# First loads of x in another order, and all five engine orders searched anew: a four-layer attention and MLP kernel on one core

## Chip, core, metric

The kernel runs on one core of a Trainium2 chip (trn2). The metric is the device time of one execution in microseconds (us). The program is one launch; nothing else runs on the core.

## What is computed

x has 2048 tokens of 448 numbers in bfloat16. Four layers follow one another, and each adds its result to x: attention, MLP, attention, MLP, with the same weights both times.

```python
def _A_ref(x, wqkv, wo):          # H = 16 heads of 28, window W = 8, dilation 2
    qkv = (x @ wqkv) -> q, k, v   # per head
    idx = pos[:, None] - arange(W)[None, :] * 2
    logits = einsum("bhsd,bhswd->bhsw", q, k[idx]) * Dh ** -0.5   # -1e9 where idx < 0
    return (softmax(logits) @ v[idx]) @ wo
def _B_ref(x, w_gate, w_up, w_down):                              # F = 1792
    return ((x @ w_gate) * (x @ w_up)) @ w_down
x = x + _A_ref(_layernorm(x), A_wqkv, A_wo)
x = x + _B_ref(_layernorm(x), B_w_gate, B_w_up, B_w_down)
x = x + _A_ref(_layernorm(x), A_wqkv, A_wo)
x = x + _B_ref(_layernorm(x), B_w_gate, B_w_up, B_w_down)
```

## The kernel before

Tokens are taken apart by parity, so that the dilation disappears: 16 blocks of 128 tokens, blocks 0 to 7 the even ones. Each layer is cut into chunks of 256 or 512 tokens, and the chunks of neighbouring layers are interleaved (`SEQ`: A00 A01 B10 A02 B11 and so on, layer and chunk).

Steps are named here by kind, layer and number. LayerNorm of a block is bn, mv (statistics, VectorE), lnv, rstd (ScalarE) and xn (normalized x, VectorE); T is its transposed form, made in layer 0's opening by a TensorE transpose (L602, L606) and a copy from PSUM on ScalarE or VectorE (L613, L616), later by a DMA. QK is the copy of a K and Q product from PSUM (L701), V and VT that of a V product. S is a group's attention scores (L826), on which an exponential (L835, ScalarE) and a minimum with a mask (L842, VectorE) follow, AV the product with V (L860), Oc and Oa its copies, Rs, Rl, R and N the division by the sum, Y the product with wo. G and H are the MLP's copy and product (L951, L954), Dd its down projection. S-2-14 is the scores of layer 2 for the group of query blocks that ends with block 14, QK-0-3-2 the copy for layer 0, chunk 3, head quarter 2.

All long matrix products go through one helper, so all have line L351. They use TensorE's array as two halves of 64 rows: two matmuls run side by side and make one pass. S and AV are bursts of 16 to 64 small matmuls; from S-0-12 on, S works on the array in columns of 32 like AV. A burst can be cut: `549*1.2.4.5/438` says that burst 549 (64 small matmuls) is cut after 8, 16, 32 and 40 of them, and that after each cut stands one step of long product 438, done as 8 strips of 32 columns (L354) in place of two matmuls, so that the array's division is the same. A number without a star is a step that runs whole. `a+b` is two bursts taken together.

Nothing chooses an order at run time. `ORDER` lists the steps of each engine by number; `BANKS` says which PSUM banks each product takes, and a product waits until the step that empties a bank has run. Waits on semaphores follow from the steps' dependences alone. The numbers are those in which `build` adds the steps, so a step added earlier or left out shifts all later numbers: after the change the numbers from 56 on are lower by 3.

At the start SyncE issues the loads of x (16 blocks; `load_x`), WV (`wv`), wqkv in four pieces (`stg`), then the MLP's weights. TensorE meanwhile runs `WARM + FILL` = 18 matmuls on zeros (L502), 13 of them ahead of the first transpose. VectorE and ScalarE copy wqkv into a padded form (L510, wqk), and a first QK product needs all eight such copies. The down-projection weights (WD) are loaded around 50 us.

Of the kernel before, what the change touches and what calls it, by code (L numbers as in the profile page):

```python
# [58 lines left out]
FILL = 9  # L59
# [36 lines left out]
def grp_nc(g):  # L96
# [21 lines left out]
    ),  # L118
    "act": (
# [12 lines left out]
    ),  # L132
    "dve": (
# [18 lines left out]
    ),  # L152
    "pool": (
        "18 19 38 20 21 22 23 24 25 26 27 28 29 30 31 32 33 34 35 36 37"
    ),
# [224 lines left out]
def build(nc, A_x, A_wqkv, A_wo, B_w_gate, B_w_up, B_w_down, out):  # L380
# [54 lines left out]
    def one(fn, key=None):  # L435
        return [(fn, key)]
# [14 lines left out]

    load_x(0, 0, 1, prio=-51.0)
    load_x(0, 1, 2, "g", -49.6)
    load_x(0, 2, 4, "h", -49.5)
    def wv_rows(a, lo, hi):
        v = A_wqkv[192 * a:192 * a + 128, lo:hi]
        r = v.ap[0][0]
# [639 lines left out]
```

## Time and profile before

| what | before |
|---|---|
| median of 3 runs, us | 384.83 (384.31 to 384.89) |
| the profiled execution, us | 383.93 |
| its span from first to last instruction, us | 382.2 |
| TensorE busy, us | 376.7 |
| VectorE busy, us | 288.2 |
| ScalarE busy, us | 203.8 |
| granted TensorE clock, mean | 1.000 |

The span is the profiled execution without the launch around it. Busy time of TensorE is modelled to the end of each matmul and these overlap, so starts are the better measure of its pace. In the chain of waits each piece is the time from its start to the start of the next piece of the chain.

### The profile page before, as it was taken

What the parts mean: (1) busy time and instruction counts of PE and PEld (TensorE: products, weight loads), DVE (VectorE), ACT (ScalarE), POOL (GpSimd) and SP (SyncE); (2) the same over time, 40 slices, a digit from 0 to 9 for tenths busy, and PEclk for the clock granted to TensorE, in tenths of its full rate; (3) what the DMA queues carried; (4) which work ended last, traced back from release to release, by engine and by line L of the source; (5) the groups of instructions that cost most, each with busy time, mean ns of one, the idle gap of its engine ahead of it and who ended that gap; (6) DMA issues with size and microseconds to landing.
All of it is one profiled execution on the core that took longest, in us unless ns stands there. A gap on an engine that the chain in (4) does not pass through costs nothing.

```text
span 382.2 us, 14253 instructions
## 1 busy us (share of the span) xinstructions
PE 376.7 (99%) x6322; PEld 211.2 (55%) x6322; DVE 288.2 (75%) x649; ACT 203.8 (53%) x388; POOL 5.2 (1%) x25
## 2 busy tenths in 40 slices
PE   8999999999999999999999999999999999999997
PEld 3545587544445445444756765545555444446664
DVE  7989999998976786787677985637998698455323
ACT  5997896756426552564465525547744635133320
POOL 5000000000000000000000000000000000000000
PEclk9999999999999999999999999999999999999999
DMA  7756454700611033031101035330125004140002
GB/s 248 196 142 160 53 121 116 84 20 2 94 32 36 2 60 62 15 67 26 32 14 34 19 44 101 36 47 4 27 34 74 3 2 66 35 116 30 3 2 98
DMA packets 54881, 22.50 MB, mean 59 GB/s; under 512 B 45012, under 2 KB 54820, under 8 KB 54820
## 3 DMA queue, kind: packets, MB, share of 16 engines
q1 hardware_dynamic: 54676, 21.53, 28.0%
q8 instruction: 50, 0.82, 0.9%
q14 instruction: 11, 0.09, 0.1%
q10 hardware_dynamic: 144, 0.06, 0.1%
HBM read 8.54 MB, written 2.71 MB: 29 GB/s over the span
## 4 chain that ended last, share of the span: by engine, by line
PE 93%; DVE 3%; ACT 1%; DMA 1%; issue 1%; SPq 0%; DVEq 0%
PE ps L351 85%; PE ps L354 3%; PE ps L860 2%; PE ps L826 2%; PE ps L966 1%; DMA x_sb<-in_A_x_dram 1%; DVE xn_sb L592 1%; ACT E_sb L835 1%; DVE Qz L812 0%; DVE R_sb L885 0%; SPq L443 0%; DVE st L571 0%; ACT xnTa L616 0%; PE ps L606 0%; ACT qk L701 0%
## 5 line engine op out<-in xcount | busy, mean ns | idle before, releaser
L351 PE MATMUL ps<-xnTb,WGU 64*128 64x512 bf16 (+1 forms) x1894 | 172.4, 332 | 0.0
L351 PEld LDWEIGHTS ps<-xnTb,WGU 64*128 64x128 bf16 x1894 | 92.3, 94 | 69.2 <-issue 1.0
L951 ACT ACTIVATE g_sb<-ps 128x512 bf16<-128x512 f32 (+1 forms) x140 | 70.2, 509 | 84.4 <-PE ps L351 64.6
L954 DVE TENSOR_TENSOR hT<-g_sb,ps 128x512 bf16<-128x512 bf16 (+1 forms) x140 | 78.2, 574 | 47.1 <-ACT g_sb L951 44.5
L351 PE MATMUL ps<-WD,hT 64*128 64x448 bf16 x812 | 82.9, 349 | 0.0
L351 PEld LDWEIGHTS ps<-WD,hT 64*128 64x128 bf16 x812 | 38.9, 94 | 34.9 <-DVE hT L954 0.4
L351 PE MATMUL ps<-xnTa,WQK 64*128 64x512 bf16 (+1 forms) x494 | 53.1, 352 | 0.4 <-ACT qk L701 0.2
L915 DVE TENSOR_TENSOR x_sb<-x_sb,ps 128x448 bf16<-128x448 bf16 x62 | 37.1, 612 | 13.6 <-PE ps L351 13.4
L835 ACT ACTIVATE E_sb<-ps,shift_sb 128x1024 bf16<-128x1024 f32 (+1 forms) x36 | 37.1, 1067 | 12.6 <-PE ps L826 12.4
L592 DVE TENSOR_SCALAR xn_sb<-x_sb,mv,rstd 128x512 bf16<-128x512 bf16 (+1 forms) x64 | 35.4, 567 | 6.4 <-ACT rstd L576 6.2
L571 DVE BATCH_NORM_STATS2 st<-x_sb 128x6 f32<-128x448 bf16 x64 | 38.5, 615 | 1.1 <-DMA x_sb<-in_A_x_dram 0.7
L351 PEld LDWEIGHTS ps<-xnTa,WQK 64*128 64x128 bf16 x494 | 23.0, 94 | 22.0 <-ACT xnTa L616 0.5
L701 ACT ACTIVATE qk<-ps 128x1024 bf16<-128x1024 f32 (+1 forms) x27 | 25.4, 958 | 16.1 <-PE ps L351 16.0
L351 PE MATMUL ps<-wo_g,oT 64*128 64x448 bf16 x250 | 28.6, 349 | 0.0
L842 DVE TENSOR_TENSOR E_sb<-E_sb,MK 128x1024 bf16<-128x1024 bf16 (+1 forms) x36 | 23.3, 658 | 5.3 <-ACT E_sb L835 5.2
L886 ACT ACTIVATE R_sb<-R_sb 128x480 f32<-128x480 f32 (+1 forms) x34 | 20.2, 600 | 11.1 <-DVE R_sb L885 10.9
L898 DVE TENSOR_TENSOR oT<-O_sb,R_sb 128x480 bf16<-128x480 f32 (+3 forms) x36 | 22.1, 624 | 4.3 <-ACT R_sb L887 4.2
L351 PE MATMUL ps<-WV,xnTa 64*128 64x336 bf16 (+3 forms) x252 | 24.0, 304 | 0.3
L885 DVE STREAM_SHUFFLE R_sb<-O_sb 128x480 f32<-128x480 f32 (+1 forms) x34 | 22.9, 693 | 0.0
L574 ACT ACTIVATE lnv<-mv,eps_sb 128x2 f32<-128x2 f32 (+1 forms) x33 | 9.3, 291 | 22.3 <-DVE mv L573 22.3
L887 ACT ACTIVATE R_sb<-R_sb 128x480 f32<-128x480 f32 (+1 forms) x34 | 20.0, 600 | 0.6
L871 ACT ACTIVATE O_sb<-ps 128x512 f32<-128x512 f32 (+3 forms) x19 | 10.4, 559 | 14.2 <-PE ps L860 14.2
(60 smaller groups left out, 217.8 us busy)
## 6 DMA issues: line engine op xcount, KB each, us to landing
out_dram<-x_sb SPq DMA_DIRECT2D x15, 112.0 KB, 1.8
x_sb<-in_A_x_dram SPq DMA_DIRECT2D x3, 448.0 KB, 6.3
hT<-in_A_wqkv_dram SPq DMA_DIRECT2D x4, 224.0 KB, 4.9
WGU<-in_B_w_gate_dram SPq DMA_DIRECT2D x4, 224.0 KB, 3.5
WGU<-in_B_w_up_dram SPq DMA_DIRECT2D x4, 224.0 KB, 4.1
WD<-in_B_w_down_dram SPq DMA_DIRECT2D x2, 448.0 KB, 4.1
WGU<-in_B_w_gate_dram SPq DMA_DIRECT2D x2, 336.0 KB, 4.5
WGU<-in_B_w_up_dram SPq DMA_DIRECT2D x2, 336.0 KB, 4.4
```

The lines of the kernel that those rows point to most:

```text
L351: return lambda E: E.matmul(out(), lhs(), rhs(), start=start, stop=stop)
L571: sc.add("dve", one(lambda E, B=B: E.bn_stats(st6[:, B, :], x_sb[:, B, :]), ("bn", li, B)), 525.0, deps=[("x", li - 1, B)] + ([("xn", li - ...
L592: sc.add("dve", one(lambda E, B=B, dst=dst, src=src: E.tensor_scalar(dst, src, mv[:, B, 0:1], rstd[:, B:B + 1], ALU.subtract, ALU.mult), ( ...
L701: return E.activation(dst, src, ACT.Copy) if hasattr(E, "activation") else E.tensor_copy(dst, src)
L835: return E.activation(E_sb[:, slot, 2 * hp:2 * hp + 2, 0:w], ps[:, b0:b0 + 2, 0:w], ACT.Exp, bias=shift_sb[:, 0:1], scale=SCALE)
L842: return E.tensor_tensor(e, e, MK[:, kind, 0:nc].unsqueeze(1).unsqueeze(1).to_broadcast([128, 2, w // nc, nc]), ALU.min)
L885: sc.add("dve", one(lambda E: E.stream_shuffle(R_sb[:, rs, 0:w], O_sb[:, os_, 0:w], [DH] * 32), ("Rs", li, qb)), dve_est(w) + 20.0, deps=[ ...
L886: sc.add("act", one(lambda E: E.activation(R_sb[:, rs, 0:w], R_sb[:, rs, 0:w], ACT.Ln), ("Rl", li, qb)), act_est(w, False), deps=[("Rs", l ...
L898: return E.tensor_tensor(oT[:, :, a % HALF:a % HALF + z - a], O[:, :, a - tok:z - tok], R_sb[:, rs, 0:w].rearrange("p (h n) -> p h n", h=4 ...
L915: sc.add("dve", one(lambda E: E.tensor_tensor(x_sb[:, B, :], x_sb[:, B, :], ps[:, bk[w], 0:D], ALU.add), ("x", li, B)), dve_est(D), deps=[ ...
L951: sc.add("act", one(lambda E, gs=gs, bk=bk: E.activation(g_sb[:, gs, 0:nt], ps[:, bk[0], 0:nt], ACT.Copy), ("G", li, j, fc)), act_est(nt), ...
L954: sc.add("dve", one(lambda E, gs=gs, bk=bk, fc=fc: E.tensor_tensor(hT[:, fc, hs, 0:nt], g_sb[:, gs, 0:nt], ps[:, bk[1], 0:nt], ALU.mult), ...
```

## The change

The first loads of x go in the order block 1, block 0, blocks 2 and 3, blocks 4 to 7 (before: 1, 2 and 3, 0, 4 to 7). Six of the filler matmuls of `FILL` remain of nine, 15 in all, 12 of them ahead of the first two transposes. The small constants' memsets are added in a fixed order, the copies `wqp` are VectorE's by declaration (they ran there before too), and `ORDER` and `BANKS` are replaced throughout by lists from a new search, which by the change's own words counted down-projection loads as delaying instruction fetches. The steps themselves are the same but for the three fillers; 19 copies move from ScalarE to VectorE and 22 the other way.

```diff
-FILL = 9
+FILL = 6
...
     "pe": (
-        "41 42 43 44 45 46 47 48 49 50 51 52 53 108 54 55 56 105 57 58 123 206 126 207 236 129 132 237 200 224 201 225 196 230 197 150 231 226 194 227 198 195 "
...
-        "352 365 353 366 498 272 499 375 369 565 370 566 569 570 397 380 304 298 301 310 284 307 285 316 322 334 313 319 392 522 331 393 402 516 325 517 328 "
-        "511 337 512 340 341 544*3.5/342 343 527 584 414 585 415 444 441 453 447 459 539 456 540 549*1.2.4.5/438 468 465 471 450 595*1.3.5/462 477 589 561 474 "
...
-        "1237 1244 1312 1334 1245 1301 1246 1238 1302 1247 1239 1401 1398 1392 1404 1351*1.3.5/1416 1324 1346 1395 1325 1347 1428 1413 1410 1422 "
...
+        "41 42 43 44 45 46 47 48 49 50 51 52 105 102 53 54 55 120 203 123 204 233 129 126 234 197 193 198 221 194 222 195 191 196 227 192 228 225 223 153 144 "
...
+        "399 541*2.4.5/339 513 340 524 581 514 582 411 438 412 444 456 536 450 537 468 462 546*1.2.4.5/441 453 435 465 447 592*1.3.5/474 459 471 477 586 478 "
...
+        "1309+1326*3.5.7.9.11.13/1235 1236 1241 1242 1331*3.5/1298 1243 1244 1299 1395 1398 1410 1348*1.3.5/1389 1321 1401 1392 1404 1322 1422 "
...
-    load_x(0, 0, 1, prio=-51.0)
-    load_x(0, 1, 2, "g", -49.6)
-    load_x(0, 2, 4, "h", -49.5)
+    load_x(0, 1, 2, "g", -51.0)
+    load_x(0, 0, 1, prio=-50.9)
+    load_x(0, 2, 4, "h", -50.8)
+    load_x(1, prio=-50.7)
...
-    memset("dve", eps_sb[:], EPS, "c_eps", 70)
-    memset("dve", wo_g[:], 0.0, "c_wo", 760)
+    first = sc.ops[-1]
+    memset("dve", eps_sb[:], EPS, "c_eps", 70, after=first)
+    memset("dve", wo_g[:], 0.0, "c_wo", 760, after=first)
...
-            sc.add(("pool", "dve"), one(fn, ("wqp", c, w)), {"pool": 240.0, "dve": 115.0}, ...
+            sc.add("dve", one(fn, ("wqp", c, w)), {"dve": 115.0}, ...
```

In the old list 1312 is AV-2-12, 1334 AV-2-14, 1329 (cut three times, in the line ahead of the one shown) S-2-14, 402 AV-0-8 and 544 S-0-12; in the new one 1309 is AV-2-12, 1326 S-2-14, 1331 AV-2-14 and 541 S-0-12, with AV-0-8 (399) right ahead of it.

The bursts whose cuts or neighbours differ, by number of cuts:

| burst | before | after |
|---|---|---|
| AV-0-8, S-0-12 | none; 2, apart | none; 3, neighbours |
| S-0-16, AV-0-16 | 3; 2 | 2; 3 |
| S-2-4 | 1 | 3 |
| AV-2-6 | 3 | 2 |
| AV-2-8 | 3 | 2 |
| S-2-14 | 3, alone | together with AV-2-12, 6 in all |
| AV-2-12, AV-2-14 | none, neighbours | see S-2-14; 2, alone |

Copies that change engines in the opening: T-0-2, T-0-7, T-0-8, T-0-10, QK-0-2-0 and VT-0-0 from ScalarE to VectorE; T-0-4, T-0-12, T-0-13, T-0-15, QK-0-0-2, QK-0-3-2 and QK-0-4-3 from VectorE to ScalarE; two weight copies and two Oc copies change places with two others of their kind. ScalarE's order after rstd of block 5 is T-0-3, two weight copies, V-0-0, T-0-5, T-0-4 (before: T-0-3, two weight copies, T-0-5, and V-0-0 five steps after that). On SyncE the four wqkv pieces go 0, 1, 2, 3 (before 0, 2, 1, 3), x 8 to 11 goes ahead of one further weight load, the ones for vt go ahead of nine weight loads, and the four WD loads go behind a few more stores to vt. GpSimd's order differs in one memset.

More of the change, by code (lines that the diff above doesn't have):

```diff
@@ L104 @@
     "pe": (
[13 rows of a table removed]
[13 rows of a table added]
     ),
     "act": (
[12 rows of a table removed]
[12 rows of a table added]
     ),
     "dve": (
[18 rows of a table removed]
[18 rows of a table added]
     ),
     "pool": (
-        "18 19 38 20 21 22 23 24 25 26 27 28 29 30 31 32 33 34 35 36 37"
+        "18 19 20 21 22 23 24 25 26 27 28 29 30 31 32 33 34 35 36 37 38"
     ),
     "sp": (
[5 rows of a table removed]
[5 rows of a table added]
     ),
@@ L446, in build, with load_x @@
     stage = hT[:].rearrange("p f s n -> p (f s n)")
-    def load_x(q, lo=0, hi=4, tag="", prio=0.0):
+    def load_x(q, lo=0, hi=4, tag="", prio=0.0, after=None):
         two, b0 = q // 2, 4 * (q % 2)
-        plain_dma("sp", x_sb[:, 4 * q + lo:4 * q + hi, :], x_par[two][:, b0 + lo:b0 + hi, :], [("x", -1, B) for B in range(4 * q + lo, 4 * q + hi)], f"d_x{q}" + tag, prio=prio)
-    load_x(0, 0, 1, prio=-51.0)
-    load_x(0, 1, 2, "g", -49.6)
-    load_x(0, 2, 4, "h", -49.5)
+        plain_dma("sp", x_sb[:, 4 * q + lo:4 * q + hi, :], x_par[two][:, b0 + lo:b0 + hi, :], [("x", -1, B) for B in range(4 * q + lo, 4 * q + hi)], f"d_x{q}" + tag, prio=prio, after=after)
+    load_x(0, 1, 2, "g", -51.0)
+    load_x(0, 0, 1, prio=-50.9)
+    load_x(0, 2, 4, "h", -50.8)
+    load_x(1, prio=-50.7)
     def wv_rows(a, lo, hi):
@@ L461, in build @@
         plain_dma("sp", stage[:, 2 * D * c:2 * D * (c + 1)], A_wqkv[CH_ROWS[c]:CH_ROWS[c] + 128, 0:2 * D], ("stg", c), f"d_stg{c}", prio=-49.9)
-    load_x(1, prio=-49.3)
     for a in range(2):
@@ L470, in build, with memset @@
     sc.add("act", one(act_table_load), 1300.0, prio=-61)
-    def memset(eng, ap, val, key, est):
-        sc.add(eng, one(lambda E: E.memset(ap, val), key), est, prio=-40)
+    def memset(eng, ap, val, key, est, after=None):
+        sc.add(eng, one(lambda E: E.memset(ap, val), key), est, prio=-40, after=after)
     memset("dve", warm, 0.0, "c_warm", 100)
-    memset("dve", eps_sb[:], EPS, "c_eps", 70)
-    memset("dve", wo_g[:], 0.0, "c_wo", 760)
+    first = sc.ops[-1]
+    memset("dve", eps_sb[:], EPS, "c_eps", 70, after=first)
+    memset("dve", wo_g[:], 0.0, "c_wo", 760, after=first)
     sc.add("pool", one(lambda E: E.memset(ident[:], 1.0), "i_id"), 150, prio=-46)
@@ L483, in build @@
     memset("pool", shift_sb[:], -SHIFT, "c_shift", 100)
-    memset("pool", MK[:], BIG, "i_mk", 300)
+    memset("pool", ones32[:], 1.0, "c_ones", 100)
+    masks_after = [o for o in sc.ops if o.engs == ("pool",)]
+    for o, prev in zip(masks_after[1:], masks_after):
+        o.after = prev
+    memset("pool", MK[:], BIG, "i_mk", 300, after=masks_after[-1])
     later = [(W - 1 - 64, 1, -1), (64, -1, 1)]
@@ L495, in build @@
     assert HALF - qb_info(STRADDLE)[0] == 64 and STRADDLE % 2 == 0
-    memset("pool", ones32[:], 1.0, "c_ones", 100)
-    sc.add("dve", one(lambda E: E.memset(qmask[:], 0.0), "i_qm"), 60, prio=-39.5)
+    sc.add("dve", one(lambda E: E.memset(qmask[:], 0.0), "i_qm"), 60, prio=-39.5, after=first)
     sc.add("dve", [((lambda E, r=r: E.memset(qmask[32 * r:32 * r + DH, r % 2:r % 2 + 1], 1.0)), "c_qm" if r == 3 else None) for r in range(4)], 240, deps=["i_qm"], prio=-39.5)
@@ L518, in fn @@
                 return E.tensor_copy(dst, src)
-            sc.add(("pool", "dve"), one(fn, ("wqp", c, w)), {"pool": 240.0, "dve": 115.0}, deps=[("stv", c // 2), "c_wqk0"] + [(k, 0, 0, cc) for k in ("Kps", "Qps") for cc in range(4)] + [(k, *NOPW[-1], cc) for k in ("Kps", "Qps") for cc in range(4)], prio=-27.5)
+            sc.add("dve", one(fn, ("wqp", c, w)), {"dve": 115.0}, deps=[("stv", c // 2), "c_wqk0"] + [(k, 0, 0, cc) for k in ("Kps", "Qps") for cc in range(4)] + [(k, *NOPW[-1], cc) for k in ("Kps", "Qps") for cc in range(4)], prio=-27.5)
     WQKR = [(k, c, w) for c in range(4) for w in range(2) for k in ("wqk", "wqp")]
```

119 rows, old and new, of tables (BANKS, ORDER) are left out of this document.

## The prediction

> **What bounds the kernel now.** I read the page first, then the busy time by stretches, then the chain of waits in order of time, and last the timeline of the first 22 us.
>
> ```profile
> span 382.2 us, 14253 instructions
> PE 376.7 (99%) x6322; PEld 211.2 (55%) x6322; DVE 288.2 (75%) x649; ACT 203.8 (53%) x388; POOL 5.2 (1%) x25
> q8 instruction: 50, 0.82, 0.9%
> PE 93%; DVE 3%; ACT 1%; DMA 1%; issue 1%; SPq 0%; DVEq 0%
> ```
>
> TensorE is busy for 376.7 of 382.2 us and holds 93% of the chain. So nearly everything that TensorE no longer does, or no longer waits for, is taken off the end, and a saving elsewhere counts only where TensorE waited for it. Line q8 matters later: 50 fetches of instructions, against 6322 matmuls and 6322 weight loads on TensorE, is one fetch for about 253 instructions of that engine.
>
> ```profile
> core 0: us, PE busy (x) PEld busy (x) DVE busy (x) ACT busy (x) POOL busy (x), PEclk, DMA share, GB/s
> 8.30:11.40 3.10, 2.90 (x61) 1.84 (x60) 3.10 (x13) 3.08 (x9) 0.00 (x0) 1.00 1.08 352
> 20.80:48.40 27.60, 26.51 (x554) 14.32 (x554) 25.95 (x67) 24.22 (x39) 0.00 (x0) 1.00 0.52 111
> 48.40:100.00 51.60, 51.60 (x1060) 32.20 (x1062) 49.25 (x114) 36.79 (x73) 0.00 (x0) 1.00 0.35 69
> 284.00:287.00 3.00, 2.46 (x140) 1.62 (x138) 2.96 (x6) 0.13 (x2) 0.00 (x0) 1.00 0.77 77
> 287.00:380.00 93.00, 92.82 (x1156) 50.56 (x1152) 54.24 (x109) 33.02 (x65) 0.00 (x0) 1.00 0.21 43
> ```
>
> The first two numbers of a row are its length and TensorE's busy time. TensorE idles in three places: a few tenths near the first QK product, 1.09 us between 20.8 and 48.4 (VectorE is busy for 25.95 of those 27.60 us and ScalarE for 24.22, so both are close to full), and 0.54 us at 284 to 287. After 287 it idles for 0.18 us in 93, with ScalarE and VectorE at a third and a little over half: what is won at 285 us reaches the end undiminished. Busy TensorE can still be slow TensorE, and that shows in the chain.
>
> **The bursts and their prices.** Attention's small matmuls (L826 scores, L860 attention times V) come in bursts of 64 and use the array in 32 columns; the long products (L351) use 128. A burst can stand alone, or be cut, with 8 strips of a long product (L354) between its pieces.
>
> ```profile
> 61.90 0.61 PE ps L860 x64
> ...
> 69.87 0.22 PE ps L826 x18
> ...
> 70.71 2.38 PE ps L351 x24
> ...
> 126.94 0.21 PE ps L860 x24
> ...
> 127.76 21.37 PE ps L351 x218
> ...
> 194.06 0.41 PE ps L826 x30
> ...
> 194.81 5.76 PE ps L351 x68
> ...
> 257.95 0.18 PE ps L860 x16
> ...
> 258.95 6.39 PE ps L351 x58
> 265.35 0.15 PE ps L860 x8
> 265.50 0.22 PE ps L354 x8
> ...
> 280.43 0.18 PE ps L826 x10
> ...
> 281.40 3.51 PE ps L351 x36
> 284.91 0.61 PE ps L860 x64
> ...
> 286.23 0.50 issue
> ...
> 286.93 13.77 PE ps L351 x140
> ```
>
> The columns are start, length, what. From a burst's first row to the next L351 row is its whole time; the strips in it are useful work, 0.22 us a step at 512 columns (row 265.50), so 0.19 at 448. What is left is the burst's price. AV alone: 0.61. AV with 3 steps: 1.00 - 0.66 = 0.34 (257.95). AV with 2: 0.82 - 0.44 = 0.38 (126.94). S with 3: 0.97 - 0.57 = 0.40 (280.43). S with 2: 0.84 - 0.38 = 0.46 (69.87). S with 1: 0.75 - 0.22 = 0.53 (194.06). Going into a burst costs again about 0.1, in the piece before it: 36 matmuls of 448 columns are 18 passes, 3.42 us at 0.19, and row 281.40 has 3.51. AV-2-12 and AV-2-14, uncut and back to back, take 284.91 to 286.93 = 2.02 us, 0.50 of which is "issue": TensorE waits in the middle of the second burst for nothing that a semaphore shows. These are 128 matmuls and 128 loads, one whole fetch of the q8 line, run in about 1.5 us; I read it as instructions that had not arrived.
>
> **The change part by part.** The new order lists hold the same long passes; I compared the bursts one by one.
>
> (a) At 280 to 287 us: before, S-2-14 cut by 3 steps, then the uncut pair: 0.40 + 2.02 + two entries of 0.10 = 2.62. After, AV-2-12 and S-2-14 are one burst cut by 6 steps, and AV-2-14 is cut by 2. No row shows AV and S in one cut burst. From above it is two bursts, 0.34 + 0.40 + 0.20 = 0.94; with one way out and one entry fewer it is 0.74, and I go 0.08 lower for the bottom (the pieces may hide more loads). I take 0.74, the sum of its two halves less one switch each way. AV-2-14: 0.38 + 0.10. After: 1.22, gain 1.40 (1.20 to 1.48).
> (b) AV-0-8 alone and S-0-12 with 2 steps, 0.61 + 0.46 + 0.20 = 1.27, become neighbours, S with 3 steps: 0.61 + 0.40 + 0.10, less the way back of 0.10, is 1.01. Gain 0.26 (0.16 to 0.36, one switch more or less).
> (c) S-2-4 goes from 1 step to 3: 0.53 to 0.40, gain 0.13.
> (d) S-0-16 goes from 3 steps to 2 (loss 0.06), AV-0-16 from 2 to 3 (gain 0.04), AV-2-6 and AV-2-8 from 3 to 2 (loss 0.08): loss 0.10.
>
> All others keep their number of cuts. Sum of the bursts: a gain of 1.69 us (1.4 to 1.9).
>
> [...]
>
> **The opening.** These rows are of the timeline and the groups by shape.
>
> ```profile
> 1.25 5.55 PE L502 MATMUL ps<-hT 128*128 128x512 bf16 x13 [1.25 <-DVE eps_sb L473]
> ...
> 4.11 1.68 DVE L571 BATCH_NORM_STATS2 st<-x_sb 128x6 f32<-128x448 bf16 x3 [0.30 <-DMA x_sb<-in_A_x_dram]
> ...
> 8.26 0.29 PE L606 MATMUL ps<-ident,xn_sb 64*128 64x64 bf16 x8
> ...
> 9.79 1.09 ACT L510 ACTIVATE WQK<-hT 128x448 bf16<-128x448 bf16 x2
> ...
> 11.42 3.58 PEld L351 LDWEIGHTS ps<-xnTa,WQK 64*128 64x128 bf16 x48 [0.54 <-ACT xnTa L616]
> ...
> 12.99 0.34 ACT L775 ACTIVATE v_sb<-ps 128x224 bf16<-128x224 f32 x1
> ...
> 13.22 0.26 ACT L780 ACTIVATE v_sb<-ps 128x112 bf16<-128x112 f32 x1
> ...
> 21.40 0.29 PEld L826 LDWEIGHTS ps<-Qz,qk 64*64 64x64 bf16 x16 [0.73 <-ACT xnTa L616]
> ```
> ```profile
> L701 ACT ACTIVATE qk<-ps 128x1024 bf16<-128x1024 f32 x23 | 23.3, 1022 | 14.1 <-PE ps L351 14.0
> ...
> L701 DVE CAST qk<-ps 128x1024 bf16<-128x1024 f32 x5 | 6.1, 1223 | 1.7 <-PE ps L351 1.5
> ...
> L616 ACT ACTIVATE xnTa<-ps 128x512 bf16<-128x512 bf16 x8 | 4.7, 596 | 0.3 <-PE ps L606 0.3
> ...
> L701 DVE CAST qk<-ps 128x512 bf16<-128x512 f32 x4 | 2.7, 682 | 0.0
> ...
> L616 DVE COPY xnTa<-ps 128x512 bf16<-128x512 bf16 x6 | 2.5, 417 | 0.0
> ```
>
> Fillers: 13 run before the first transpose, 0.43 us each; three fewer free TensorE for 0.3 us at most where it waits for normalized x anyway. I count nothing.
>
> Loads of x: with block 0 second, VectorE no longer waits 0.30 us at 4.11 before its statistics; the eps and qmask memsets move behind and fill part of that. The weights that QK needs come after the same bytes as before (x 0 to 7, then WV, then the four pieces), so the first QK product cannot come earlier. On SyncE, pieces 1 and 2 change places, x 8 to 11 passes one weight load, the ones for vt move ahead of nine loads, and the down-projection loads move behind more vt stores: all are needed tens of us later, and the cover is that distance. GpSimd's ones memset moves behind four others, in 5.2 us of work that ends by 7.
>
> First QK: ScalarE's order is now two weight copies, V of block 0, then the transposes T-0-5 and T-0-4. In times of before: 10.88 after the weight copies (9.79 + 1.09), 11.48 after V (0.34 + 0.26), 12.08 after T-0-5. QK's first piece takes V's bank at 11.5, three passes of 256 columns (0.33) later the next piece needs T-0-5's bank and waits from 11.8 to 12.1. Against 11.42 and no such wait before, this loses 0.3.
>
> S-0-0, the wait at 21.40: there ScalarE is late with a transpose's copy. It loses T-0-2, T-0-7, T-0-8 and a 0.26 us V copy and takes T-0-4 and a 512-column QK copy (0.68 on VectorE, no more here): about 0.8 us less before that point, enough to make up the 0.3. I put both at 0 together; the bounds are a gain of 0.4 and a loss of 0.3.
>
> 21 to 48 us: over the opening VectorE gives away T-0-4, T-0-12, T-0-13, T-0-15, QK-0-0-2, QK-0-3-2 and QK-0-4-3 (4 x 0.417 + 2 x 0.682 + 1.223 = 4.26) and takes T-0-2, T-0-7, T-0-8, T-0-10, QK-0-2-0 and a V copy (4 x 0.417 + 1.223 + about 0.3 = 3.19). So 1.07 us leave VectorE, and 0.9 comes to ScalarE (QK-0-0-2 and QK-0-4-3 at 0.6 each as for 512 columns in row 596, QK-0-3-2 against QK-0-2-0 at 1.022 each, less 0.26), which had 3.38 us free in 20.8 to 48.4 against VectorE's 1.65. TensorE idles 1.09 there; I take 0.3 of it as won. Bounds: a gain of 1.1 (all the idle goes), a loss of 0.9 (ScalarE becomes the late one).
>
> **Sum.** -1.69 + 0 - 0.3 = -2.0 us on the profiled execution: span 382.2 to 380.2. That execution took 383.93, and the median of the three runs is 384.83, 0.9 above; I take 2.0 off the median: **382.8**.
>
> **Rivals.** (B) The bursts gain, and the opening gives it back: ScalarE takes VectorE's place as the late engine, +0.9 and +0.3, which leaves -0.5: 384.3. For it: both engines are over 87% busy in 20.8 to 48.4. Against: the wait at 21.40 is on ScalarE, and there it gets less work.
>
> (C) Slower, at 6 to 12 us: with three fillers fewer TensorE stands idle for some 0.7 us around 7.6 (12 fillers from 1.25 end at 6.4, two transposes and three fillers make 7.6, and block 2's transpose did not start before 8.26), and its clock, which rises only during the fillers (13 took 0.43 us each, twice a 512-column step's 0.22), does not rise or falls back. The work at 8.3 to 11.4, 2.90 us, then takes up to 2.9 more. With -2.0 that is +0.9: 385.7. It decides from 2.8 us of lost time on. Against: the waits between fillers and transposes were there before too. [...]
>
> (D) Slower, in 48 to 284 us: the old order leaves TensorE no idle time there at all (51.60 of 51.60 us in the row above), so a new order can only add waits. Eight to ten new ones of 0.3 us, the size of the waits quoted, are 2.8 us: +0.8, 385.6. For it: every list changes. Against: VectorE and ScalarE have slack there after 100 us, and the order of stages is the same.
>
> (E) The fetch comes back: the merged burst is 128 small matmuls and 48 strips with as many loads, 352 instructions in 0.74 + 6 x 0.19 = 1.9 us, denser than one fetch allows if a block's edge falls badly. Price 0.5 to 0.9: 383.3 to 383.7, still faster; it belongs to the forecast's own range, 381.6 to 384.0.
>
> **Chances.** Forecast with E 0.60, B 0.22, C 0.08, D 0.10. A measurement of this kernel can tell 0.2%, 0.77 us, from no change. So faster by more than that 0.60, within it 0.22 (B), slower 0.18 (C and D). The range goes from the forecast's lower end, 381.6, over B to the edge of D, 385.5.
>
> **What would show it.** Right: no "issue" of 0.5 us in the chain near 285, a single stretch of L860, L826 and L354 for AV-2-12 and S-2-14 of about 1.9 us, and 1.3 us or more won between the row of 280 us and the end; TensorE idle in 20.8 to 48.4 under 1.09 us. Wrong: fillers or the first V passes at 0.43 us after 7 us (C); idle TensorE between 48 and 284 (D); S-0-0 or S-0-8 later than 21.4 and 48.4 (B); an "issue" row inside the merged burst (E).

## The result and the profile after

The changed kernel takes 385.85 us (median of 18 runs, 385.29 to 388.42) where the kernel before takes 384.76 (18 runs on the same chip, 384.0 to 386.16): ratio 1.0037, 95% interval 1.0026 to 1.0049. It is slower by 1 to 1.9 us; 2.0 faster was forecast. Its profiled run is the longest of the 18, so a second trace of the same kernel (run *again* below, 385.14 us) is read beside it.

The page of the profiled run, its busy lines and the chain's shares:

```profile
span 386.7 us, 14316 instructions
PE 378.0 (98%) x6355; PEld 209.5 (54%) x6355; DVE 286.5 (74%) x646; ACT 204.7 (53%) x391; POOL 5.2 (1%) x25
PE 92%; DVE 3%; DMA 2%; ACT 2%; SPq 1%; issue 1%; DVEq 0%
```

DMA and SyncE's queue now hold a part of the chain, and TensorE idles more. Where, by the busy time by stretches, first of the profiled run, then of *again* (length, TensorE busy):

```profile
20.80:48.40 27.60, 24.77 (x520) 12.86 (x520) 22.55 (x59) 22.75 (x36) 0.00 (x0) 1.00 0.49 115
48.40:100.00 51.60, 50.79 (x1068) 31.78 (x1066) 48.53 (x112) 35.12 (x70) 0.00 (x0) 1.00 0.35 72
100.00:284.00 184.00, 183.11 (x3096) 99.77 (x3094) 135.01 (x290) 95.01 (x179) 0.00 (x0) 1.00 0.22 37
```
```profile
20.80:48.40 27.60, 26.66 (x551) 14.14 (x554) 24.43 (x63) 24.62 (x38) 0.00 (x0) 1.00 0.48 115
48.40:100.00 51.60, 50.83 (x1058) 31.58 (x1058) 48.66 (x112) 35.22 (x71) 0.00 (x0) 1.00 0.36 74
100.00:284.00 184.00, 183.86 (x3110) 100.12 (x3108) 135.22 (x291) 93.96 (x177) 0.00 (x0) 1.00 0.22 37
```

Between 48 and 100 us, where the kernel before had no idle time, TensorE idles 0.8 us in both. In 20.8 to 48.4 the two traces of one kernel differ by 1.9.

Idle time misses short losses inside "busy" stretches, and orders that differ can't be set side by side step by step. But at many points both orders have run exactly the same set of TensorE steps. The start of the next product there, changed minus before, gives the loss of each stretch, and the rows add up to the end:

| stretch, us of before | forecast | profiled run | *again* |
|---|---|---|---|
| to 26.6 | 0 | -0.17 | -0.28 |
| 26.6 to 41.1 | -0.3 | +2.68 | +0.79 |
| 41.1 to 74.1, with (b) | -0.26 | -0.35 | -0.37 |
| 74.1 to 93.2 | 0 | +0.83 | +0.71 |
| 93.2 to 203, with (c) | -0.11 | +1.88 | +0.74 |
| 203 to 276 | +0.08 | +0.37 | +0.38 |
| 276 to 294.5, with (a) | -1.40 | -1.09 | -1.10 |
| 294.5 to the end | 0 | +0.32 | +0.32 |
| sum | -2.0 | +4.47 | +1.19 |

Most of the gain forecast for the bursts came, 1.1 us of 1.40 for (a) alone; the 0.3 us forecast for 21 to 48 us did not. The losses were not forecast. Three of them can be read in chains. First the profiled run before Y-0-0, then SyncE's DMA issues in it and in *again* (start, length):

```profile
34.45 3.42 DMA wo_g<-in_A_wo_dram
37.87 0.09 issue
37.96 2.13 PE ps L351 x24
```
```profile
28.39 0.60 SPq L443 DMA_DIRECT2D WGU<-in_B_w_up_dram  x1
31.50 2.25 SPq L443 DMA_DIRECT2D wo_g<-in_A_wo_dram  x3
33.79 0.61 SPq L443 DMA_DIRECT2D WGU<-in_B_w_up_dram  x1
34.45 0.58 SPq L443 DMA_DIRECT2D wo_g<-in_A_wo_dram  x1
```
```profile
28.30 1.23 SPq L443 DMA_DIRECT2D wo_g<-in_A_wo_dram  x3
30.21 0.60 SPq L443 DMA_DIRECT2D WGU<-in_B_w_up_dram  x1
30.86 0.58 SPq L443 DMA_DIRECT2D wo_g<-in_A_wo_dram  x1
```

The last quarter of wo stands behind a weight load that waits for an earlier load to land. In *again* it is issued at 30.86 and is there in time; in the profiled run at 34.45, it lands 3.42 us later, and TensorE stands still for over 2 us. Same order, 3.6 us apart. In *again* the chain before Y-0-0 is on ScalarE:

```profile
32.80 0.49 ACT R_sb L891
33.30 0.49 ACT R_sb L890
33.79 0.62 ACT v_sb L797
34.41 0.49 ACT R_sb L891
34.90 0.92 ACT qk L705
...
35.96 2.13 PE ps L351 x24
```

Third, *again* from AV-0-8 to the product for Y-0-6:

```profile
68.38 0.75 PE ps L864 x64
...
69.15 1.03 ACT O_sb L875 x2
...
70.19 2.12 ACT E_sb L839 x2
72.31 0.99 ACT R_sb L890 x2
...
73.32 1.10 ACT R_sb L891 x2
74.42 0.93 ACT O_sb L875 x2
...
75.48 2.61 PE ps L351 x23
```

AV-0-8 now stands right ahead of S-0-12, so its copies and divisions and S-0-12's exponential follow one another on ScalarE: 1.03 + 2.12 + 0.99 + 1.10 + 0.93 = 6.17 us, and 6.3 us with the short pieces between them (69.15 to 75.48). TensorE's own steps behind AV-0-8 are done at 74.96, after 5.8 us, so it waits 0.5 us. The last term copies AV-0-10 out of the bank that the product needs.

The merged burst came as one stretch, as forecast (chain of the profiled run):

```profile
288.32 0.21 PE ps L864 x24
...
290.08 0.14 PE ps L830 x18
290.22 4.27 PE ps L351 x44
294.48 0.21 PE ps L864 x24
...
295.33 1.76 PE ps L351 x17
```

AV-2-12 and S-2-14 are one stretch of 1.90 us with six strip steps of 0.19 and no "issue" in it: a price of 0.76 without the entry, where 0.64 was forecast. AV-2-14 takes 0.85; its two strip steps are of a product of 336 columns, 0.14 each by their columns, which leaves 0.57 where 0.38 was forecast.

### The profile page after: what moved, and what is told of

The parts are those of the page before. It is cut to its first block, busy times and chain, and to the rows that moved or that the text cites. A ratio compares the mean times of both kernels' runs of the same rounds, so it can differ in the third digit from the quotient of the medians.

```text
span 386.7 us, 14316 instructions
## 1 busy us (share of the span) xinstructions
PE 378.0 (98%) x6355; PEld 209.5 (54%) x6355; DVE 286.5 (74%) x646; ACT 204.7 (53%) x391; POOL 5.2 (1%) x25
## 4 chain that ended last, share of the span: by engine, by line
PE 92%; DVE 3%; DMA 2%; ACT 2%; SPq 1%; issue 1%; DVEq 0%
PE ps L351 83%; PE ps L354 3%; PE ps L830 2%; PE ps L864 2%; PE ps L970 1%; DMA wo_g<-in_A_wo_dram 1%; SPq L443 1%; DMA x_sb<-in_A_x_dram 1%; DVE st L575 1%; ACT E_sb L839 1%; DVE R_sb L889 0%; PE ps L610 0%; DVE E_sb L846 0%; DVE xn_sb L596 0%; DVE qk L705 0%
## 5 line engine op out<-in xcount | busy, mean ns | idle before, releaser
L575 DVE BATCH_NORM_STATS2 st<-x_sb 128x6 f32<-128x448 bf16 x64 | 37.5, 614 | 1.6 <-DMA x_sb<-in_A_x_dram 1.2
L596 DVE TENSOR_SCALAR xn_sb<-x_sb,mv,rstd 128x896 bf16<-128x896 bf16 (+1 forms) x64 | 34.9, 567 | 3.0 <-ACT rstd L580 2.0
L705 ACT ACTIVATE qk<-ps 128x1024 bf16<-128x1024 f32 (+1 forms) x29 | 26.8, 936 | 13.6 <-PE ps L351 13.4
L351 PE MATMUL ps<-WV,xnTa 64*128 64x336 bf16 (+3 forms) x248 | 23.2, 304 | 0.1
L351 PEld LDWEIGHTS ps<-wo_g,oT 64*128 64x128 bf16 x252 | 12.1, 94 | 13.1 <-issue 2.4
```

What stands on the lines that cost most here:

```text
L351: return lambda E: E.matmul(out(), lhs(), rhs(), start=start, stop=stop)
L575: sc.add("dve", one(lambda E, B=B: E.bn_stats(st6[:, B, :], x_sb[:, B, :]), ("bn", li, B)), 525.0, deps=[("x", li - 1, B)] + ([("xn", li - ...
L596: sc.add("dve", one(lambda E, B=B, dst=dst, src=src: E.tensor_scalar(dst, src, mv[:, B, 0:1], rstd[:, B:B + 1], ALU.subtract, ALU.mult), ( ...
L705: return E.activation(dst, src, ACT.Copy) if hasattr(E, "activation") else E.tensor_copy(dst, src)
```

## The experiments

For kernels made of parts, `X|t|Y` says that all engines keep X's order up to the TensorE step at time t and Y's from there; the joints were put where both have run the same set of steps, and banks were renamed to fit. b is before, a the changed kernel. Ratios are to before, run alternately on the same chip.

**again**: the changed kernel unaltered.

> The changed kernel once more, unaltered, for a second trace of it. Its 18 runs spread from 385.3 to 388.4 us, and its profiled run was the longest of them. Queue theory (the load of wo's last quarter waits on SyncE behind a gated load of the MLP's weights, and TensorE waits 2.3 us for it before Y-0-0): the wait is there again, 1 to 2.5 us long, and what differs between runs of 385.3 and 388.4 is mostly its length. Fetch theory (the order is denser, so blocks of 256 instructions come late near 200 us): the issue rows of 0.7 and 0.3 us come and go instead, and the wait before Y-0-0 stays at 2.3. Median 385.9 by both.

385.14 to 387.27, median 386.55, ratio 1.0055 (1.0039 to 1.0070). Counted from start to start, 0.39 us are lost right before Y-0-0 against 2.27 in the profiled run (the view of waits has 0.22 and 2.11), and the "issue" near 200 us is 0.10 against 0.72 and 0.12: both vary from run to run, so neither theory holds alone. The profiled run's two rows of "issue" there stand 256 TensorE instructions apart (counted under fillers, below). The profiled 388.42 is the kernel with both.

**a_wo**: wo's last quarter ahead of the gated load, ones for vt last.

```diff
-"sp": "... 79 78 72 81 80 87 85 86 82 88 84 83 294 ..."
+"sp": "... 79 78 81 80 87 85 86 88 82 84 83 72 294 ..."
```

> The changed kernel with two moves on SyncE alone: the fourth wo load ahead of the gated weight load instead of behind it, and the ones for vt behind the last weight load, as before. Queue theory: the wait of 2.3 us before Y-0-0 goes, to 0.3 or less, and of that 1.5 to 2.3 us reach the end: 383.6 to 384.4. Rival, new waits spread over 48 to 284 us are what costs: the time won at 36 us is waited for again at the next tight places (AV-0-4, S-0-8), at most 0.5 us reaches the end: 385.4 or more.

385.43 (385.08 to 386.13), ratio 1.0036 (1.0023 to 1.0049), 1.1 us under *again* at overlapping intervals. All four wo loads go at 29.64 and nothing is left of the DMA wait; Y-0-0 still comes 0.39 us late, behind ScalarE. Without the DMA wait the slow end of the spread is gone: the eleven runs of a_wo and a_wo18 (below) lie in 385.08 to 386.13, where *again* reaches 387.27. Most of the loss is elsewhere, as the rival had it.

**b_wo**: the same in reverse, in the kernel before.

```diff
-"sp": "... 79 82 81 84 83 90 91 89 88 85 86 87 75 297 ..."
+"sp": "... 79 82 81 75 84 83 90 88 89 85 91 87 86 297 ..."
```

> The kernel before with the same part of the change alone: on SyncE the ones for vt ahead of nine loads, and the wo loads in the changed order, the fourth behind the gated weight load. Queue theory: TensorE waits 1.5 to 2.5 us before Y-0-0, and the median goes from 384.8 to 386.3 to 387.2. Rival (the wait came from the other engines' orders): under 385.2.

384.41, ratio 1.0001 (0.9992 to 1.0011): nothing. The last wo load went at 33.2 and Y-0-0 began at 36.7 without a wait. In the old order two more halves of products stand ahead of Y-0-0, and the changed order comes to it at 35.6: it brings Y-0-0 forward *and* its load back. My theory of SyncE alone fell.

**Which stretch?** Four kernels of parts: `b|243|a`, `b|48|a|243|b`, `a|48|b`, `a|28|b`.

```diff
-every list = changed
+b243_a:      before up to 1074, changed from 1125   (243 us)
+b48_a243_b:  changed only from 397 (S-0-8, 48 us) to 1125
+a48_b:       changed up to 397
+a28_b:       changed up to 250 (AV-0-2, 28.6 us)
```

> The kernel before up to the product that follows S-2-8 (243 us), the changed order from there on, on all engines; banks of the second part renamed so that each product finds the bank it expects. It holds the merged burst of AV-2-12 and S-2-14, the cut AV-2-14, the cuts of AV-2-8 and the changed order of the last 140 us. Theory that each stretch's waits are its own: set step by step against before, the second trace of the changed kernel loses 0.3 us from 243 to 277, wins 1.1 from 276 to 295 and loses 0.3 after it, so 0.5 us faster than before. Rival, what is won at 285 us is there only because the changed kernel arrives late with its copies done: within 0.2 us of before. As predicted for the burst alone: 1.3 us faster.

383.96, ratio 0.9991 (0.9978 to 1.0004). Step by step +0.24 at 243 to 267, -1.11 at 276 to 294.5, +0.33 after: the same as in *again*, at another place in time.

> The kernel before up to S-0-8 (48 us) and from 243 us on, the changed order between. It holds AV-0-8 next to S-0-12, three cuts in S-2-4 and all new orders of this stretch, and none of the opening. Own-waits theory: by the second trace of the changed kernel, +0.7 at 74 to 93 us, +0.3 to 145, +0.8 to 252, less 0.4 at 41 to 74: 1.3 us slower than before. Rival, the waits there are caused by the opening (ScalarE and VectorE enter the stretch with other arrears): within 0.3 us of before.

385.78, ratio 1.0037 (1.0024 to 1.0051): 1.5 us slower, as much as the whole change. Its steps are -0.1 to 74 us, +0.81 to 93, +0.32 to 145, +0.44 to 203, as in *again*; and before Y-0-6 stands the same chain of ScalarE, behind an opening that is not the changed one. The waits belong to this stretch's order.

> The changed kernel up to S-0-8 (48 us), the order before from there on. It holds the loads of x in the new order, the 15 fillers, the copies that change engines, and SyncE's new order with the wo load behind the gated weight load. Own-waits theory with the wo wait: 0.4 us slower than before in runs in which the wo load comes in time and up to 2.4 slower in the others, so a median 0.5 to 1.5 us above and a wide spread (2 us from lowest to highest). As predicted: 0.3 us faster.

383.86 (383.38 to 385.89), ratio 0.9989 (0.9974 to 1.0005). The wide spread was there, the loss not: the opening is even or slightly a gain. The three parts (-0.0011, +0.0037 and -0.0009 of the time) add up to +0.0017 where a_wo has +0.0036; the intervals are too wide to say that this differs.

> The changed kernel up to AV-0-2 (28.6 us), the order before from there on, the wo loads too. It holds the loads of x, the fillers and the first half of the moved copies. Own-waits theory: 0.2 us faster than before (the changed kernel is 0.2 to 0.3 us ahead at this point in all its traces), and no wait before Y-0-0. Rival, the lead of 0.2 is lost at once because VectorE and ScalarE carry other arrears: 0.2 to 0.5 us slower.

384.69, ratio 1.0007 (0.9994 to 1.0020): undecided. Its trace was late from 8 us on (block 2 waited 1.04 us for normalized x) and lost 0.5 at the joint. How late x comes differs between runs: at 19 us the traces with the old opening lie up to 1.1 us behind the profiled run of before, so no opening is judged by one trace.

**The wait before Y-0-6.** `b|60|a|76|b`, then the reverse in a_wo (`a|50|b|74|a`), then the move alone, by hand, in before:

```diff
-"pe": "... 393 402 516 325 517 328 ... 340 341 544*3.5/342 343 527 584 414 ..."
+"pe": "... 393 325 328 ... 340 341 402 544*2.4.5/342 516 343 527 584 517 414 ..."
 "act": 403 404 (copies of AV-0-8) behind 513, ahead of 545 546 (exponential); 407 408 411 412 behind
```

> The kernel before, with the changed order of all engines from 60 us (behind S-0-10) to 76 us (ahead of Y-0-6's second half) alone: AV-0-8 next to S-0-12, its copies on ScalarE between those of S-0-10 and the exponential of S-0-12. Theory that this place is the cause of the longest new wait: 0.2 us won by 74 us, then TensorE waits 0.7 to 0.8 us for ScalarE before Y-0-6, and in all 0.5 to 0.6 us slower than before: 384.8 to 384.9 where before is 384.3. Rival, the wait comes from arrears that ScalarE brings from the opening or from the order behind 76 us: no such wait here, 0.2 us faster by the cut: 384.1.

387.02, ratio 1.0061 (1.0046 to 1.0076), but 1.6 us of it are one wait for a bank at the second joint.

> The changed kernel with the wo loads put right, and from 50 to 74 us the order before on all engines, so AV-0-8 stands where it stood. The same theory: the wait before Y-0-6 is gone (under 0.2 us), and with the cut's 0.2 us given up it is 0.5 us faster than the kernel with the wo loads alone: 384.9. Rival: the wait stays, 385.4.

389.68, ratio 1.0123 (1.0106 to 1.0141): again a bank at a joint (2.5 us). These two say nothing on the place of AV-0-8.

> The kernel before with AV-0-8 moved behind the product ahead of S-0-12, S-0-12 with three cuts, the V product 12 behind the burst, and the copies of AV-0-8, the exponential of S-0-12 and the divisions on ScalarE in the order of the change (copies, exponential, divisions); no joints. Theory that this place costs the wait before Y-0-6: ScalarE has 6.2 us of work between the end of AV-0-8 and the copies that Y-0-6 waits for (copies 1.0, exponential 2.1, divisions 2.1, copies 0.9), TensorE 5.5, so TensorE waits 0.7 to 1.1 us there; with 0.2 to 0.4 won on the bursts the kernel is 0.3 to 0.9 us slower than before: 384.6 to 385.2. As predicted (b): 0.26 us faster: 384.1.

388.98, ratio 1.0112 (1.0094 to 1.0130). Of its trace's chain:

```profile
69.85 0.80 PE ps L860 x64
...
70.67 1.03 ACT O_sb L871 x2
71.70 2.06 ACT E_sb L835 x2
...
75.41 0.61 ACT R_sb L887
...
76.04 0.73 DVE oT L898 x2
76.77 0.60 DVE E_sb L842
77.37 0.54 DVE x_sb L915
...
77.96 6.14 PE ps L351 x59
```

The chain runs again from AV-0-8 through copies, exponential and divisions; TensorE waited 2.1 us at its end (1.9 by the view of waits), 1.1 of them for VectorE steps that my hand-made order put behind. The two shortest of its five runs, the traced one among them, have a mean granted clock of 1.000, the other three of 0.996, so a part of the median's loss is clock. Another 1.3 us went at 63 us: with AV-0-8 gone from there, the next product waits for a bank. So the chain is seen in every trace with AV-0-8 at the new place and, joints aside, in none with it at the old one. What it costs is shown only together with the rest of the order around it: from 60.2 to 75.4 us the five traces with the changed order there (the profiled run, *again*, a_wo, a_wo18, b48_a243_b) lose 0.47 to 0.62 us against before, those with the old order there (b_wo, a48_b, b243_a, combo, mix, mix3) between -0.07 and +0.02.

**The merged burst alone**, in before, in three tries: only the burst; with AV-2-12's copies ahead of the exponential's mask; with the third copy moved as well.

```diff
-"pe": "... 1233 1329*2.4.5/1236 1237 1244 1312 1334 1245 1301 1246 1238 1302 1247 1239 1401 ..."
+"pe": "... 1233 1236 1237 1312+1329*3.5.7.9.11.13/1238 1239 1244 1245 1334*3.5/1301 1246 1247 1302 1401 ..."
-"dve": "... 1381 1386 1384 1333 1332 1388 1314 1313 1315 1316 1390 1320 1323 1319 1303 1337 1350 1342 ..."
+"dve": "... 1381 1386 1314 1313 1315 1384 1388 1390 1333 1332 1316 1320 1319 1323 1337 1350 1303 1342 ..."   (b_burst3)
```

> The kernel before with the bursts near 285 us as in the change: AV-2-12 and S-2-14 as one burst with six cuts, AV-2-14 with two. As predicted: the 0.50 us of issue goes, 1.4 us are won on TensorE, nothing after it waits: 383.4. Rival 1, only the cuts gain and the missing fetch shows elsewhere in the same or the next block: 0.9 us, 383.9. Rival 2, S-2-14 comes 3.5 us later, and its exponential and AV-2-14 now hold TensorE up: 384.8 or more, with a wait after 290 us.

391.91, ratio 1.0203 (1.0190 to 1.0216). TensorE waits 4.1 us at once for the bank of AV-2-12:

```profile
PE ps L351 <- DVE O_sb L875: 5.2, 2, 4.1
```

> The kernel before with the merged burst of AV-2-12 and S-2-14 and the cut AV-2-14, and this time the copies of AV-2-12 ahead of the exponential's mask on VectorE, and the divisions of AV-2-12 ahead of AV-2-14's copies on ScalarE, as the change has them. As predicted: 1.4 us faster, 382.9. By the step between 276 and 295 us in the traces of the changed kernel: 1.1 us faster, 383.2. Rival, the burst can't be had without waits behind it: 383.8 or more, with TensorE waiting between 286 and 310 us.

387.89, ratio 1.0104 (1.0081 to 1.0126); the same wait, 2.2 us.

> The kernel before with the merged burst and the cut AV-2-14 as in b_burst2, and three further moves on VectorE: the last of AV-2-12's copies (it frees the bank for which TensorE waited 2.4 us there) right behind the other two, and that of AV-2-14 ahead of the copy of a V product that comes later. As predicted for the burst: 1.4 us faster, 382.9. By the step between 276 and 295 us in five traces with the changed order: 1.1, less 0.25 for a wait before the second part of the product ahead of the burst, 0.85 us faster: 383.4. Rival: the gain is eaten by waits behind the burst again: 383.9 or more.

384.75, ratio 1.0022 (1.0004 to 1.0040). One wait is left, for the copy of a V product (columns: total, times, longest):

```profile
PE ps L351 <- DVE v_sb L793: 1.1, 1, 1.1
```

From 274.7 to 294.5 us it loses 0.46; of that 1.24 is this wait and its entry and 0.25 one ahead of the burst, so the burst itself wins 1.03. In these three tries it can't be had alone: the copies on VectorE and ScalarE have to move with it.

**Fillers.** Before with 15, and a_wo with 18.

```diff
-FILL = 9
+FILL = 6          (b_fill15; a_wo18 the reverse)
```

> The kernel before with 15 fillers in place of 18, and nothing else. As predicted: no difference, 384.3. Fetch theory: six instructions fewer stand ahead of every later block of 256, the uncut pair AV-2-12 and AV-2-14 at 285 us falls otherwise on the blocks, and its waits of 0.6 to 0.9 us become 0.2 to 0.4, as in both kernels that have the changed opening and this pair: 383.8. Clock theory (the fillers' pause lets the clock fall): up to 2.9 us slower, with V products of 0.43 us a pass after 8 us.

385.38 (384.08 to 386.83), ratio 1.0020 (1.0006 to 1.0035): slower, by neither theory. In the traced run the clock stays at 1.00 and the V passes at their length; the two longest of the twelve runs (386.66 and 386.83) have a mean granted clock of 0.996. The trace loses 1.2 us before 11.4 us, where TensorE waits 0.47 and 1.39 us for normalized x, but b60_a76_b with its 18 fillers lost 1.1 there too. That the missing fillers made it slower is not shown. The stall in the uncut pair did not shrink, it moved. In the kernel before it stands ahead of the pair's last three matmuls, which with their weight loads are six instructions; with six instructions fewer ahead of it, it stands right behind the pair:

```profile
286.83 0.68 PE ps L860 x64
287.50 0.73 issue
288.24 3.80 PE ps L351 x39
```

So it sits at a fixed place in the stream of instructions. Counting TensorE's instructions (weight loads, matmuls and waits on semaphores, from zero, the three of the start included) shows more. Seven stalls that nothing visible ends, 0.50 us in before, 0.73 here, 0.40 in b_wo, 0.18 in b48_a243_b, 0.26 in b_av8, 0.72 and 0.12 in the profiled run, stand each right behind an instruction whose number leaves 193 when divided by 256: 10433 in the first five runs, 6849 and 7105 in the profiled run. A run has some 50 such places, and queue q8 moves 50 packets of instructions in it; before shows a stall of 0.1 us or more at one of these places behind 26 us, the profiled run at two. That fits instructions that had not arrived, which stays my reading: what holds TensorE there no trace shows.

> The changed kernel with the wo loads put right and with 18 fillers again: one more ahead of the first transposes, two more ahead of the third. As predicted, fillers cost and save nothing: 385.4, as with 15. If 15 fillers are what made the kernel before slower by 0.8 us: 384.6. If the three fillers stand in the way of transposes whose x is there: up to 0.6 us slower, 386.

385.40 (385.30 to 385.58), ratio 1.0031 (1.0020 to 1.0042): as a_wo with 15. That fillers cost nothing holds in the changed opening; why before was slower with three fewer stays open.

**Putting together what won.** combo is `a_wo|48|b|267|a|294|b`; mix is `a_wo|48|b|243|a`; mix3 is `a_wo|48|b_burst3`.

```diff
-every list = changed
+combo: changed only to 48 us and from 267 to 294 us
+mix:   before only from 397 (48 us) to 1074 (243 us)
+mix3:  changed to 397, then b_burst3
```

> What won, put together: the changed opening to S-0-8 with the wo loads put right, the order before from 48 to 267 us, the changed order from 267 to 294 (the merged burst), the order before from there on. Own-waits theory: the opening's 0.2 us and the burst's 1.1 us add up, 1.3 us faster than before: 383.0. Rival, a part's gain exists only with its own surroundings (other banks are held at the joints): 384 or more.

392.04, ratio 1.0184 (1.0166 to 1.0201): 3.2 us of waiting for a copy at the joint at 267 us.

> The changed kernel up to S-0-8 (48 us) with the wo loads put right, the order before from there to 243 us, the changed order from 243 us on: all of the change but the stretch in which its new waits stand, with joints at which every product finds the banks it expects. Own-waits theory: the gains of both ends add, 0.4 and 0.3 us by the medians measured for each, 0.7 us faster than before: 383.6. Rival, gains at the opening are taken up by the next stretch: 384.0 or more.

383.77 (383.42 to 384.24), ratio 0.9985 (0.9976 to 0.9994): the one version whose interval lies below that of before, by 0.6 us; the changed kernel (ratio 1.0037) lies about 2 us above it. TensorE idles 0.12 us from 48.4 to 100 where *again* idles 0.77:

```profile
48.40:100.00 51.60, 51.48 (x1062) 31.91 (x1060) 49.18 (x113) 37.33 (x74) 0.00 (x0) 1.00 0.29 68
```

> The changed opening to S-0-8 with the wo loads put right, and b_burst3's order from there on. If gains add: 0.2 us of the opening and what b_burst3 shows, 383.1 to 383.3, under the 383.8 of mix, which loses 0.6 us to waits of the changed order after 243 us. Rival: not under mix's 383.8.

384.64, ratio 1.0013 (0.9998 to 1.0027): b_burst3's last wait (1.2 us) is still in it.

## Why the prediction was wrong, point by point

**48 to 284 us: the step that failed.** The forecast's sum had no term for this stretch. Rival D had the mechanism ("a new order can only add waits"), with 2.8 us in eight to ten waits; it got a chance of 0.10 because "the order of stages is the same". Measured: 0.71 + 0.74 + 0.38 = 1.8 us between 74 and 276 in *again*, and 1.5 us as a kernel of its own (b48_a243_b); with the old order in this stretch and the changed one around it, mix is 0.6 us faster than before. One wait of 0.5 us, the one before Y-0-6, is the largest piece. From 93 to 276 us the 1.1 us went in pieces of 0.1 to 0.2 us inside busy stretches (0.16 at the product for Y-0-14 at 145 us, 0.16 at a V product at 191.8 us), and their causes stay open. The row of 51.60 busy in 51.60 was the warning: a stretch without any idle time is one in which every moved step must be followed to the engine that comes after it. (b) priced AV-0-8's move on TensorE alone. Its 0.26 came nearly whole: between 60.2 and 74.1 us 0.24 is won in *again* and 0.22 in the profiled run. But 0.7 went right behind it, most of it in the wait for ScalarE, whose five entries stand one behind the other in the order lists: that wait could have been foreseen.

**SyncE: "all are needed tens of us later, and the cover is that distance".** Wrong for wo, and the prediction's list of SyncE's moves leaves out that wo's last quarter went behind a gated weight load. In the kernel before, the loads went from 27.96 to 29.4 and Y-0-0 used them at 36.2: a cover of 7 us, not tens. The change takes 1.5 (*again*) to 5 us (profiled run) of it on SyncE, where each gated load waits for the landing of another (seven such waits by 40 us in the profiled run, the longest 5.7 us), and TensorE is at Y-0-0 by 35.6, 1.1 us earlier than in b_wo. The half on SyncE alone costs nothing (b_wo); both together cost 0 to 2 us, by run.

**21 to 48 us: -0.3 forecast, +0.3 without the wo wait.** Rival B's mechanism is there: the copies that moved to ScalarE make it the late engine at 32.8 to 35.8 (chain above), and *again* loses 0.79 us by 41.1. But it wins 0.53 of that back by S-0-8, which starts at 48.34 us where before has 48.36, and TensorE idles 0.94 us in 20.8 to 48.4 where before has 1.09. So B's sign, a later S-0-0 or S-0-8, did not come without the wo wait, nor did its price of 0.9; and neither did the gain. From 26.6 to 48.4 us *again* loses 0.26. Another 0.4 goes in short waits from 48.4 to 52 us, so the row of 41.1 to 74.1 holds -0.53, +0.4 and the -0.24 of (b). B's mechanism and D's came together, which I had not counted as a case.

**The opening to 26.6 us.** Forecast 0; -0.2 to -0.3 here, and more against the other traces of the old opening, which start later. S-0-0 and the first QK gave no new loss. C fell: from 6.9 to 11.4 us the granted clock is 1.00 in the profiled run, and its groups of V matmuls take 0.47, 1.12 and 0.92 us where before has 0.46, 1.12 and 0.93. That the clock rises during the fillers no run shows: in before they go from 0.43 us each to 0.22 (three from 6.86 to 7.51 us), and the granted clock reads 1.00 from the first of them on.

**(a), forecast 1.40.** 1.10 in the changed order, 1.03 in b_burst3 with its two waits taken off. The term that was mis-sized is the after side: 0.76 for 0.64 and 0.57 for 0.38 are the 0.3 that lack. The 0.38 came from a burst with longer strips; that strips of 336 columns hide less is my reading of this one comparison. The before side was uncertain as well: the 0.50 of "issue" was one draw, and the same pair shows 0.40 in b_wo, 0.73 with 15 fillers (above), 0.18 in b48_a243_b and none in a48_b:

```profile
285.03 1.29 PE ps L864 x128
286.32 5.78 PE ps L351 x61
```

From 276 to 294.5 us a48_b, with the old order there, takes 0.59 us less than the profiled run of before. So about half of the 1.10 is the stall, and against a run without it the new bursts win 0.5.

That two bursts can run out of instructions was my reading of the q8 line and of one row of 0.50 us; the runs show where such stalls stand (fillers, above), not their cause. Nor do they show that down-projection loads delay instructions, as the search counted: SyncE issues these loads from 50.6 to 57.0 us in before and from 54.0 to 61.1 in the profiled run, and the earliest of the seven stalls is at 200.47 us. Nor is the stall gone for good: the profiled run has a stall of this kind at a place where neither *again* nor before has one.

```profile
200.47 0.72 issue
```

**(c), forecast 0.13.** S-2-4 takes 0.75 with one step and 1.05 with three, a price of 0.39 and a gain of 0.14. It came, and the row of 93.2 to 203 hides it behind larger losses.

**After 294.5 us.** Nothing forecast, +0.32 in all traces with the changed end, from b243_a to mix. In *again* 0.19 of it is lost by 297.5 us, in one product of the MLP (1.69 us where before has 1.51), and 0.16 behind the start of the last product; the cause stays open.

## What to carry to other kernels

Where an order is changed throughout, price the order first and the improvement second: take the stretches in which the bound engine has no idle time, and add up, for each step that moved, the work that now stands in a row on the engine behind it. A load's cover is the distance from its issue to its first use, less what both ends move and less the spread between runs; look it up for each. And let a profiled stall of a few tenths without a releaser count as a range down to nothing, since the uncut pair showed 0.73 us of it in one run here, 0.18 in another and none in a third.

## What the runs showed of the hardware

In three traces the granted clock of TensorE fell behind a wait, of 2.53, 3.2 and 4.12 us. First awo_b50_b74, then b_burst2: the first product after the wait (timeline; the wait is in the brackets) and the stretches behind it (the granted clock is the third number from the end).

```profile
79.09 1.58 PE L351 MATMUL ps<-wo_g,oT 64*128 64x448 bf16 x8 [2.53 <-DVE x_sb L919]
```
```profile
79.00:83.00 4.00, 3.91 (x22) 1.53 (x24) 0.63 (x2) 0.00 (x0) 0.00 (x0) 0.57 0.08 18
83.00:87.00 4.00, 4.00 (x40) 1.81 (x38) 2.66 (x5) 2.78 (x5) 0.00 (x0) 1.00 0.02 4
```
```profile
289.31 2.82 PE L351 MATMUL ps<-WD,hT 64*128 64x448 bf16 x28 [2.23 <-DVE O_sb L875]
```
```profile
289.30:293.00 3.70, 3.69 (x112) 2.12 (x114) 2.54 (x6) 2.30 (x4) 0.00 (x0) 1.00 0.33 65
```

After 2.53 us TensorE works for 4 us at 0.57 of its clock, so by my estimate (0.43 of 4.00 us) the wait costs 1.7 us more than its length. After the waits of 3.2 us in combo and 4.12 us in b_burst the clock falls too, to 0.64 over 4.7 us and 0.55 over 3.8 us. After 2.23 us it doesn't fall in b_burst2's trace (1.00 over 3.7 us), nor after the wo wait of 2.1 us in the profiled run (1.00 from 38 to 41 us). The runs give no fixed length at which it happens: one of the six runs of b_burst2 (390.59 us) and three of the five of b_av8, whose longest wait in the trace is 1.9 us, show a mean granted clock of 0.996, as the trace of awo_b50_b74 does, and two of the five runs of awo_b50_b74 show 1.000. Whether the waits were longer in those runs is not known.
